# Issuing 64-row matmuls as two 64-column halves: a fused convolution and gated feed-forward kernel on one core

## The chip, the cores and the metric

The kernel runs on one core of a Trainium2 chip (trn2). The metric is the device time of one execution in microseconds. The kernel before takes 711.89 us, the median of two runs (711.63 and 712.15). One further execution was profiled. Engines are named as in the profile: PE is TensorE's matmuls, PEld its weight loads, DVE is VectorE, ACT is ScalarE, POOL is GpSimd, SP is SyncE, which here starts most transfers.

## What is computed

The input is x of 8 sequences by 4096 positions by 192 channels in fp32. First comes a causal convolution of 7 taps; the 192 channels fall into 8 heads of 24, and all channels of a head share 7 softmaxed taps. Its result, seen as 32768 tokens by 192, goes through a feed-forward layer with 2048 hidden units:

```
w   = softmax(weight, axis=-1)                        # 8 heads x 7 taps
a   = einsum('hk,bskhg->bshg', w, windows of 7 of x)  # causal, zero padded
h   = a.reshape(32768, 192) @ moe_w_in                # 192 x 2048
g   = h * cos(h)
out = g @ moe_w_out                                   # 2048 x 192, fp32
```

## The kernel before, in words

Everything is unrolled in Python, with the order of the instructions written out by hand (`manual_schedule`). Tokens are worked on in 64 tiles of T = 512 (index t); the convolution works in units of U = 1024 (index u), two tiles each. All matmul operands are bf16, and sums are fp32 in PSUM.

A matmul here has a stationary operand (`lhsT`, put into the array by a weight load, LDWEIGHTS) and a moving operand (`rhs`, streamed through). In almost all of the kernel a matmul uses only 64 of the array's 128 rows and all 128 columns. They come in pairs, one on rows 0 to 63 and one on rows 64 to 127, which write different PSUM banks. Such a pair is called a step below. There are three products made in this way:

- The convolution as a band matrix (`conv_mm`, L193, called by `conv_part`, L220). For units 3 and up each part is 8 matmuls of 64 rows, streaming 192 columns; units 1 and 2 use full 128-row matmuls through the same helper. Unit 0 has code of its own (`conv_first` L338, `conv_rest` L373), which the diff doesn't touch; it issues 128 by 128 matmuls that stream 48 columns (L347) or 96 (L379).
- The first layer (`mm1`, L402, matmul at L411). 192 channels are 3 blocks of 64. For each tile and each of 8 pairs j of hidden blocks there are 3 steps: k runs over the blocks, i over the two row halves, each half with its own hidden block and its own bank of the PSUM tile `h`. Each matmul streams 512 columns. ACT then takes the cosine (L419, by sine with a shift) and DVE multiplies (L423) into the SBUF tile `g`.
- The second layer (`mm2_step`, L430, matmul at L458). The stationary operand is a 64-row slice of `g` for 128 tokens, the moving one 64 rows of `wo` (192 columns). There are 64 steps per tile, and each step's two matmuls write the two banks of `o_ps`. After half of them the row halves change banks, with a `Turn` between (L163): `mark` puts a no-operation on SP's queue that depends on the last matmuls of the first half, and `wait` makes the first matmuls of the second half depend on it, so that two row halves never write one bank together. `conv_part` uses the same device.

The order on PE is a string for each tile, walked by the loop at the end. In the steady state it is

```
PE_ORDER = "m11 h0 m4 h1 m6 h2 m7 q Y K h3 m7 h4 m7 c1 m4 c2 X L m5 h5 m9 p h6 D O h7 m4"
```

where `h3` is the first-layer product j = 3, `m7` is seven steps of the second layer (of the tile before, mostly), and `c1`, `c2` are the two pieces of a convolution part. The other letters issue work on other queues: L loads x, K casts it, D doubles and X transposes by DMA, Y mends the edges of a unit, O stores. ACT and DVE follow in an order of their own (`ACT_ORDER`). PSUM's eight banks are all in use: three `h` tiles of two banks, and one bank each for `o_p` and `o_q`.

At the start PE is kept at work on a zero tile (`keep_warm`, L107) while the band matrix is built; after the first unit, PE runs the three products in turn until the end.

Of the kernel before, what the change touches and what calls it, by code (L numbers as in the profile page):

```python
# [16 lines left out]
def kernel(  # L17
# [8 lines left out]
    nc = tc.nc  # L26
# [3 lines left out]
    G = D // H  # L30
# [11 lines left out]
    NC = D // 64  # L42
# [37 lines left out]
    w = consts.tile([128, NC, NP, 128], BF16)  # L80
# [28 lines left out]
            nc.tensor.matmul(out=bank, lhsT=zero[:, 0:128], rhs=zero, start=True, stop=True)  # L109


    quarter = consts.tile([4, 128], FP32)
    nc.gpsimd.memset(quarter, 1.0)
    nc.gpsimd.affine_select(out=quarter, in_=quarter, compare_op=ALU.is_ge, fill=0.0, base=0, pattern=[[1, 128]],
# [19 lines left out]
    band = consts.tile([128, H, 256], BF16)  # L134
# [23 lines left out]
    wo = consts.tile([128, NP, 2, D], BF16)  # L158
# [18 lines left out]
    bf = {}  # L177
# [15 lines left out]
    def conv_mm(u, c, ps, i, rows, n0, n1, prev=0, **flags):  # L193

        h = 4 * c + i
        return nc.tensor.matmul(  # L196
            out=ps[i // 2][:, 0 : (n1 - n0) * 2 * G].rearrange("p (n k i r) -> p i n k r", n=n1 - n0, k=NC, i=2)[:, i % 2],
            lhsT=band[rows, h, 128 if prev else 0 : 256 if prev else 128],
            rhs=bf[u][rows, n0:n1, h * G : (h + 1) * G].rearrange("p n (k r) -> p n k r", k=NC),
            skip_group_check=True, **flags)  # L200

    def conv_out(u, c, ps, n0, m0, m1, copy, double=False, banks=(0, 1)):

        for b in banks:
            w0 = (2 * c + b) * 2 * R
            o = ct_tiles[u][:, m0:m1, :, :, w0 : w0 + 2 * R].rearrange("p n k t w -> p (n k) t w")
            i = ps[b][:, (m0 - n0) * 2 * G : (m1 - n0) * 2 * G].rearrange("p (m t w) -> p m t w", t=1, w=2 * R)
            if double:
                copy(o, i.to_broadcast([128, (m1 - m0) * NC, 2, 2 * R]))
            else:  # L210
                copy(o[:, :, 0, :], i[:, :, 0, :])  # L211

    def ring_banks():
        h = h_pool.tile([128, 2, T], FP32, name="h")
        return [h[:, 0, :], h[:, 1, :]]
# [4 lines left out]
    def conv_part(u, c, banks, whole=False):  # L220


        ps = banks()
        nb = UB + (u == 1)
        sides = [slice(0, 64), slice(64, 128)]

        def mm(i, rows, **flags):
            return conv_mm(u, c, ps, i, sides[rows], 0, nb, **{"start": False, "stop": False, **flags})

        if whole:  # L230
            for i in range(4):
                conv_mm(u, c, ps, i, slice(0, 128), 0, nb, start=i % 2 == 0, stop=i % 2 == 1)
            if u == 2 and c == 0:
                spread_taps(ps[1][:, UB * 2 * G : UB * 2 * G + K])
            yield
        else:
            mm(0, 0, start=True)
            mm(2, 1, start=True)
            turn = Turn()
            turn.mark(mm(1, 0), mm(3, 1))  # L240
            yield
            turn.wait(mm(2, 0), mm(0, 1))
            mm(3, 0, stop=True)
            mm(1, 1, stop=True)
        yield
        if u not in ct_tiles:
            ct_tiles[u] = ct_pool.tile([128, UB + 1, NC, 2, 64], BF16, name="ct")
        for b in range(2):
            conv_out(u, c, ps, 0, 0, nb, nc.scalar.copy, banks=(b,))
            if b and u == 2 and c == 0:  # L250
                nc.scalar.copy(tap, ps[1][:, UB * 2 * G : UB * 2 * G + K])
            if b:
                have.add(("conv", u, c))
            yield
# [28 lines left out]
    def spread_taps(ps):  # L283

        for i in range(2):
            nc.tensor.matmul(out=ps, lhsT=pick[:, i].rearrange("p t q i r -> p (t q i r)"), rhs=wn[:, i, :],
                             start=i == 0, stop=i == 1, skip_group_check=True)
# [40 lines left out]
    for i, k in enumerate("DPDPDPDPDPDPDPAA"):  # L328
        q, rows = divmod(i, 4)
# [69 lines left out]
    g_tiles = {}  # L399
    o_state = {}  # L400

    def mm1(t, j, n0=0, n1=NB):  # L402

        assert ("whole", t // TPU, t % TPU) in have
        c = cT[t // TPU]
        m0 = (t % TPU) * NB
        h = h_pool.tile([128, 2, T], FP32, name="h")
        for k in range(NC):
            for i in range(2):
                rows = slice(64 * i, 64 * i + 64)  # L410
                nc.tensor.matmul(out=h[:, i, n0 * 128 : n1 * 128], lhsT=w[rows, k, j, :], rhs=c[rows, m0 + n0 : m0 + n1, k, :],  # L411
                                 start=(k == 0), stop=(k == NC - 1))
        return h

    def gcu(t, j, h, n0=0, n1=NB):
# [14 lines left out]
    def mm2_step(q):  # L430
        tt, i = divmod(q, 2 * STEPS)
        half, k = divmod(i, STEPS)
        if tt >= NT:
            return
        if tt < NT - 1:
            f, si = divmod(k, 2)
            if i == 0:
                for b in range(2):
                    bank = o_pools[b].tile([128, T], FP32, name="o_ps%d" % b)
                    for j in range(2):  # L440
                        o_ps[tt, b, j] = bank[:, j * D : (j + 1) * D]
                    o_ps[tt, b] = bank[:, 0 : 2 * D]
            first, last = i == 0, i == 2 * STEPS - 1
        else:

            si, f = divmod(k, NF) if half else LAST_HALF[k]
            if half == 0 and f == 0:
                bank = [o_pools[b].tile([128, T], FP32, name="o_ps%d" % b) for b in range(2)] if si else ring_banks()
                for b in range(2):
                    o_ps[tt, b, si] = bank[b][:, 0:D]  # L450
            first, last = half == 0 and f == 0, half == 1 and f == NF - 1
        assert ("wo", f // 2 // HP) in have and {("g", tt, f // 2, s) for s in (2 * half + si, 2 * (1 - half) + si)} <= have
        ms = []
        for r in range(2):
            b = half ^ r
            rows = slice(64 * r, 64 * r + 64)
            s = 2 * b + si
            ms.append(nc.tensor.matmul(out=o_ps[tt, b, si], lhsT=g_tiles[tt][rows, f, s * 128 : (s + 1) * 128],  # L458
                                       rhs=wo[rows, f // 2, f % 2, :], start=first, stop=last, skip_group_check=True))
        if tt < NT - 1:  # L460
            if i == STEPS - 1:
                turns[tt] = Turn()
                turns[tt].mark(*ms)
            if i == STEPS:
                turns.pop(tt).wait(*ms)
        elif f == NF - 1 and half == 0:
            turns[tt, si] = Turn()
            turns[tt, si].mark(*ms)
        elif f == 0 and half == 1:
            turns.pop((tt, si)).wait(*ms)  # L470
# [18 lines left out]
    o_ps, o_sb, turns, evacs = {}, {}, {}, set()  # L489
# [21 lines left out]
    for v in (1, 2, 3):  # L511
        for i, part in enumerate("dc"):
            conv[part, v] = conv_part(v, i, ring_banks, v < 3)
    step, made, stored, done = 0, -1, 0, set()
    for t in range(NT + 1):
        u, second = divmod(t, TPU)
        cu = u + TPU
        if t >= 2 * TPU:
            conv["c"] = conv_part(cu, second, ring_banks) if cu < NU else iter(())
        pe = PE_LAST if t == NT - 1 else "m%d p" % (2 * STEPS * NT - step) if t == NT else PE_ORDER if t >= len(PE_FIRST) else PE_FIRST[t]  # L520
        act = ACT_LAST if t == NT - 1 else ACT_ORDER if t >= len(ACT_FIRST) else ACT_FIRST[t]
        act, h = act.split(), {}
# [35 lines left out]
        for k in pe.split():  # L558
            if k[0] == "h":
                if t < NT:  # L560
                    h[k[1:]] = mm1(t, int(k[1]), *HALVES[k[2:]])
            elif k[0] in "rdc":
                next(conv[part_of(k)], None)
            elif k[0] == "m":
                for q in range(step, step + int(k[1:])):
                    mm2_step(q)
                step += int(k[1:])
            elif k[0] == "w":
                keep_warm(int(k[1:]), o_pools[0].tile([128, T], FP32, name="o_ps0"))
            elif k == "p":  # L570
                assert step % (2 * STEPS) == 0
                made = step // (2 * STEPS) - 1
            elif k == "q":
                assert step % (2 * STEPS) == STEPS
            elif k[0] == "W":
                cast_wo(int(k[1]))
            elif k == "O":
                while stored <= made and (stored, 0) in evacs and (stored, 1) in evacs:
                    store(stored)
                    stored += 1  # L580
            elif k[1:]:
                of_unit(k[0], int(k[1]))
            else:
                v = {"D": cu, "X": u + 1, "Y": u + 1, "K": u + 3, "L": u + 4}[k]
                if t >= 2 * TPU and v < NU and (k in "DLY") == bool(second):
                    of_unit(k, v)
# [35 lines left out]
```

## Time and profile before

| what | value |
|---|---|
| median of the runs | 711.89 us |
| the profiled execution's own time | 711.61 us |
| its span in the profile | 709.9 us |
| mean granted TensorE clock | 0.999 |
| instructions in the span | 26545 |
| busy DVE, ACT, POOL | 637.5, 599.8, 304.2 us |

The span is the time from the program's first instruction to its last, and 1.7 us lie around it. PE's share of busy time is not a measure of how well it is used: a matmul's record is longer than the time after which the next can start, so records overlap and the row reads full even if they come less often. What counts is how far apart they start. The chain view gives that best: it lists runs of instructions of one kind with their number and the time until the next kind. In the lists of instructions the time given with several merged ones runs from the first start to the last end, so that the spacing is that time less one record, divided by one less than the number. "x14" is a count, and "64x192" the moving operand's rows by columns; "64*128" is rows by columns of the stationary operand.

### The profile page before, as it was taken

The numbers are of one execution on the slowest core, as the hardware profiler recorded it, in microseconds if no ns is written. First come the engines' busy times: TensorE is split into PE (matmuls) and PEld (weight loads), VectorE is DVE, ScalarE is ACT, GpSimd is POOL, SyncE is SP. The second block draws the span as 40 slices with busy tenths as digits, with TensorE's granted clock in tenths as the row PEclk, the third lists the DMA queues.
The fourth block names the chain that finished last, engine by engine and source line by source line (L and its number), as shares of the span: only waits on it lengthen the run. The fifth ranks groups of instructions, "written<-read, shape, count | busy, mean of one in ns | idle before, by whom it ended". The sixth has DMA issues, their size and how long they took to land.

```text
span 709.9 us, 26545 instructions
## 1 busy us (share of the span) xinstructions
PE 703.0 (99%) x11836; PEld 537.6 (76%) x11838; DVE 637.5 (90%) x598; ACT 599.8 (84%) x719; POOL 304.2 (43%) x308
## 2 busy tenths in 40 slices
PE   8999999999999999999999999999999999999997
PEld 4677777777777777777777777777777777777776
DVE  6889998998998999899999989989989999999996
ACT  7888888888888888888888888888888888888875
POOL 6653355333454433553434554335544335532400
PEclk9999999999999999999999999999999999999999
DMA  8954535535445455355354365553454554543411
GB/s 210 252 137 96 116 106 146 126 93 147 100 120 147 101 120 140 94 134 142 80 145 117 104 146 119 103 145 101 122 146 91 129 125 104 139 96 75 96 46 46
DMA packets 183713, 85.25 MB, mean 120 GB/s; under 512 B 111664, under 2 KB 183216, under 8 KB 183600
## 3 DMA queue, kind: packets, MB, share of 16 engines
q1 hardware_dynamic: 182888, 82.59, 47.9%
q8 instruction: 92, 1.51, 0.9%
q0 software_dynamic: 416, 0.79, 0.7%
q10 hardware_dynamic: 296, 0.20, 0.1%
q14 instruction: 21, 0.17, 0.1%
HBM read 31.36 MB, written 25.17 MB: 80 GB/s over the span
## 4 chain that ended last, share of the span: by engine, by line
PE 96%; DMA 1%; DVE 1%; POOL 0%; ACT 0%; SPq 0%; issue 0%; POOLq 0%
PE o_ps L458 47%; PE h L411 46%; PE h L196 3%; DMA x_f<-in_x_dram 1%; DVE g L423 0%; ACT cs L419 0%; PE h L458 0%; SPq L75 0%; POOL x_bf L184 0%; POOL mask L132 0%; PE o_ps L109 0%; ACT mask L137 0%; DVE diag L319 0%; DVE prod L316 0%; DVE o_sb L486 0%
## 5 line engine op out<-in xcount | busy, mean ns | idle before, releaser
L423 DVE TENSOR_TENSOR g<-h,cs 128x1024 bf16<-128x1024 f32 (+1 forms) x513 | 599.9, 1217 | 19.9 <-ACT cs L419 17.1
L419 ACT ACTIVATE cs<-h 128x1024 bf16<-128x1024 f32 (+1 forms) x513 | 514.4, 1022 | 85.1 <-PE h L411 64.9
L458 PEld LDWEIGHTS <-g 64*128 64x128 bf16 x8192 | 368.9, 94 | 91.6 <-DVE g L423 0.4
L458 PE MATMUL o_ps<-wo,g 64*128 64x192 bf16 x8128 | 434.8, 243 | 0.0
L411 PE MATMUL h<-cT,w 64*128 64x512 bf16 (+1 forms) x3078 | 412.2, 376 | 0.6 <-DVE g L423 0.3
L411 PEld LDWEIGHTS <-w 64*128 64x128 bf16 x3078 | 160.3, 94 | 67.4 <-issue 1.6
L302 POOL TENSOR_TENSOR edge_prod<-cT,tap 128x1008 f32<-128x1008 bf16 x30 | 67.2, 2241 | 281.7 <-DMA cT<-ct 281.7
L184 POOL CAST x_bf<-x_f 128x1728 bf16<-128x1728 f32 (+2 forms) x33 | 80.8, 2448 | 60.5 <-DMA x_f<-in_x_dram 42.3
L476 DVE COPY o_sb<-o_ps 128x384 f32<-128x384 f32 x62 | 34.6, 558 | 42.8 <-PE o_ps L458 42.6
L211 ACT CAST ct<-h 128x384 bf16<-128x384 f32 (+1 forms) x124 | 53.8, 484 | 14.0 <-PE h L196 13.4
L264 POOL COPY ct<-ct 128x1536 bf16<-128x1536 bf16 (+1 forms) x31 | 45.6, 1470 | 14.1 <-ACT ct L211 11.5
L196 PE MATMUL h<-x_bf,band 64*128 64x192 bf16 (+2 forms) x480 | 42.1, 243 | 0.1
L307 POOL TENSOR_TENSOR edge_prod<-edge_prod 128x144 f32<-128x144 f32 x60 | 33.3, 555 | 4.7
L305 POOL TENSOR_TENSOR edge_prod<-edge_prod 128x432 f32<-128x432 f32 x30 | 30.3, 1010 | 2.4
L476 ACT COPY o_sb<-o_ps 128x384 f32<-128x384 f32 x64 | 30.2, 474 | 0.1
L196 PEld LDWEIGHTS <-band 64*128 64x128 bf16 (+1 forms) x480 | 22.8, 94 | 1.5 <-issue 1.3
L308 POOL TENSOR_TENSOR cT<-edge_prod 128x144 bf16<-128x144 f32 x30 | 18.3, 610 | 2.4
L266 POOL COPY ct<-x_bf 128x192 bf16<-128x192 bf16 x60 | 19.2, 350 | 0.0
L109 PE MATMUL o_ps<-zero 128*128 128x512 bf16 x20 | 6.8, 476 | 1.4 <-DVE zero L104 1.3
L109 PEld LDWEIGHTS <-zero 128*128 128x128 bf16 x24 | 2.3, 110 | 4.2 <-issue 2.1
L93 POOL CAST wo<-wo_f 128x1536 bf16<-128x1536 f32 x2 | 2.9, 1469 | 2.4 <-DMA wo_f<-in_moe_w_out_dram 2.4
L458 PE MATMUL h<-wo,g 64*128 64x192 bf16 x64 | 3.2, 244 | 0.1
(61 smaller groups left out, 35.5 us busy)
## 6 DMA issues: line engine op xcount, KB each, us to landing
out_dram<-o_sb SPq DMA_DIRECT2D x63, 384.0 KB
x_f<-in_x_dram SPq DMA_DIRECT2D x30, 768.0 KB
x_f<-in_x_dram SPq DMA_DIRECT2D x31, 96.0 KB
x_f<-in_x_dram SPq DMA_DIRECT2D x4, 384.0 KB
wo_f<-in_moe_w_out_dram SPq DMA_DIRECT2D x4, 384.0 KB
w<-in_moe_w_in_dram POOLq DMA_DIRECT2D x2, 384.0 KB, 6.2
cT<-ct SPq DMA_TRANSPOSE x32
out_dram<-o_sb ACTq DMA_DIRECT2D x2, 96.0 KB
```

Of the source, the lines that this page charges most:

```text
L184: copy(out=bf[u][:, n0 + o : n1 + o, :].rearrange("p n (h k r) -> p (n h) k r", k=NC, r=R), in_=x_tiles[u][:, n0:n1, :].rearrange("p n (h ...
L196: return nc.tensor.matmul(out=ps[i // 2][:, 0 : (n1 - n0) * 2 * G].rearrange("p (n k i r) -> p i n k r", n=n1 - n0, k=NC, i=2)[:, i % 2], ...
L211: copy(o[:, :, 0, :], i[:, :, 0, :])
L264: nc.gpsimd.tensor_copy(out=ct[:, 0:nb, :, 1, :], in_=ct[:, 0:nb, :, 0, :])
L302: nc.gpsimd.tensor_tensor(out=edge_prod, in0=window, in1=tap.rearrange("p (a b k) -> p a b k", a=1, b=1).to_broadcast([128, NC * UB, K - 1 ...
L305: nc.gpsimd.tensor_tensor(out=edge_prod[:, :, :, 0:3], in0=edge_prod[:, :, :, 0:3], in1=edge_prod[:, :, :, 3:6], op=ALU.add)
L307: nc.gpsimd.tensor_tensor(out=edge_prod[:, :, :, 0], in0=edge_prod[:, :, :, 0], in1=edge_prod[:, :, :, j], op=ALU.add)
L411: nc.tensor.matmul(out=h[:, i, n0 * 128 : n1 * 128], lhsT=w[rows, k, j, :], rhs=c[rows, m0 + n0 : m0 + n1, k, :], start=(k == 0), stop=(k ...
L419: nc.scalar.activation(out=cs[:, :, part], in_=h[:, :, part], func=AF.Sin, bias=math.pi / 2.0, scale=1.0)
L423: nc.vector.tensor_tensor(out=g_tiles[t][:, 2 * j : 2 * j + 2, part], in0=h[:, :, part], in1=cs[:, :, part], op=ALU.mult)
L458: ms.append(nc.tensor.matmul(out=o_ps[tt, b, si], lhsT=g_tiles[tt][rows, f, s * 128 : (s + 1) * 128], rhs=wo[rows, f // 2, f % 2, :], star ...
L476: (copy or copies[b])(o_sb[t][:, 2 * b : 2 * b + 2, :].rearrange("p s d -> p (s d)"), o_ps.pop((t, b)))
```

## The change

A helper issues a matmul as two, on columns 0 to 63 and 64 to 127 of the stationary operand, writing partitions 0 to 63 and 64 to 127 of the same PSUM region; both stream the same moving operand. All three products call it. A step of two matmuls and two weight loads becomes four matmuls and four weight loads, each on a quarter of the array. The lists handed to `Turn` grow from two instructions to four. Nothing else changes: the order, the buffers, the transfers and the other engines' work stay.

```diff
+    COLS = [slice(0, 64), slice(64, 128)]
+
+    def halves_mm(out, lhsT, rhs, **flags):
+
+        return [nc.tensor.matmul(out=out[c], lhsT=lhsT[:, c], rhs=rhs, skip_group_check=True, **flags) for c in COLS]
...
     def conv_mm(u, c, ps, i, rows, n0, n1, prev=0, **flags):
 
         h = 4 * c + i
-        return nc.tensor.matmul(
-            out=ps[i // 2][:, 0 : (n1 - n0) * 2 * G].rearrange("p (n k i r) -> p i n k r", n=n1 - n0, k=NC, i=2)[:, i % 2],
-            lhsT=band[rows, h, 128 if prev else 0 : 256 if prev else 128],
-            rhs=bf[u][rows, n0:n1, h * G : (h + 1) * G].rearrange("p n (k r) -> p n k r", k=NC),
-            skip_group_check=True, **flags)
+        return halves_mm(
+            ps[i // 2][:, 0 : (n1 - n0) * 2 * G].rearrange("p (n k i r) -> p i n k r", n=n1 - n0, k=NC, i=2)[:, i % 2],
+            band[rows, h, 128 if prev else 0 : 256 if prev else 128],
+            bf[u][rows, n0:n1, h * G : (h + 1) * G].rearrange("p n (k r) -> p n k r", k=NC), **flags)
...
-            turn.mark(mm(1, 0), mm(3, 1))
+            turn.mark(*mm(1, 0), *mm(3, 1))
             yield
-            turn.wait(mm(2, 0), mm(0, 1))
+            turn.wait(*mm(2, 0), *mm(0, 1))
...
-                nc.tensor.matmul(out=h[:, i, n0 * 128 : n1 * 128], lhsT=w[rows, k, j, :], rhs=c[rows, m0 + n0 : m0 + n1, k, :],
-                                 start=(k == 0), stop=(k == NC - 1))
+                halves_mm(h[:, i, n0 * 128 : n1 * 128], w[rows, k, j, :], c[rows, m0 + n0 : m0 + n1, k, :],
+                          start=(k == 0), stop=(k == NC - 1))
...
-            ms.append(nc.tensor.matmul(out=o_ps[tt, b, si], lhsT=g_tiles[tt][rows, f, s * 128 : (s + 1) * 128],
-                                       rhs=wo[rows, f // 2, f % 2, :], start=first, stop=last, skip_group_check=True))
+            ms += halves_mm(o_ps[tt, b, si], g_tiles[tt][rows, f, s * 128 : (s + 1) * 128], wo[rows, f // 2, f % 2, :],
+                            start=first, stop=last)
```

## The prediction

> **What bounds the kernel now.** I read the page first (engines, clock, groups, instruction queue), then the chain of waits in a steady stretch, then the list of instructions where PE issues most densely.
>
> ```profile
> PE 703.0 (99%) x11836; PEld 537.6 (76%) x11838; DVE 637.5 (90%) x598; ACT 599.8 (84%) x719; POOL 304.2 (43%) x308
> ...
> PEclk9999999999999999999999999999999999999999
> ...
> q8 instruction: 92, 1.51, 0.9%
> ...
> L458 PEld LDWEIGHTS <-g 64*128 64x128 bf16 x8192 | 368.9, 94 | 91.6 <-DVE g L423 0.4
> L458 PE MATMUL o_ps<-wo,g 64*128 64x192 bf16 x8128 | 434.8, 243 | 0.0
> L411 PE MATMUL h<-cT,w 64*128 64x512 bf16 (+1 forms) x3078 | 412.2, 376 | 0.6 <-DVE g L423 0.3
> ```
>
> PE stands idle before its two big groups for 0.0 and 0.6 us in 709.9, at full clock throughout. Busy alone proves little, since a record (243 or 376 ns) is longer than the spacing. The chain gives the spacing, first as a whole, then in a window:
>
> ```profile
> 128.82 1.29 PE h L411 x12
> 139.61 1.29 PE h L411 x12
> ...
> 665.28 1.32 PE o_ps L458 x32
> ```
>
> ```profile
> 130.12 1.24 PE o_ps L458 x30
> 131.36 0.65 PE h L411 x6
> ```
>
> 32 matmuls of L458 are 16 steps in 1.32 us, 82.5 ns for a step that streams 192 columns (15 steps in 1.24 agree). 6 of L411 are 3 steps in 0.65 us, about 216 ns for 512 columns. The same place of the order comes round after 139.61 - 128.82 = 10.79 us, one tile: 24 steps of L411, 64 of L458 and 4 of L196. 68 x 82.5 = 5.61 us leave 5.18 for the 24, 215.8 ns each. The difference is 133.3 ns for 320 columns, 0.4166 ns each; so 512 columns are 213.3 ns, 192 are 80.0, and each step has 2.5 ns on top. The two row halves stream side by side, at one column per 0.4166 ns each, and all 128 columns of the array are in use. The period holds nothing but steps: PE's streaming is the bound, and the weight loads (94 ns each as recorded) are fully under it.
>
> Over the whole kernel there are 3072 / 2 = 1536 steps of L411 and 8192 / 2 + 464 / 2 = 4328 steps of 192 columns (L458 and L196). 1536 x 215.8 + 4328 x 82.5 = 331.5 + 357.1 = 688.6 us; the other 21.3 us of the span are start and end. The profiled execution took 711.6 us, 0.3 below the median of the runs, so sums against it hold for the median too.
>
> **The change, part by part.**
>
> *Streaming.* Removed: 11728 matmuls in 5864 steps. Added: 23456, four to a step, each on a quarter of the array, each streaming as many columns as before. If the four stream side by side as the two do now, a step costs what it did, 215.8 or 82.5 ns: nothing won, nothing lost. No row shows two column halves at work, so the ends are: below nothing, the fixed 2.5 ns of a step gone (-14.7 us); above, the column halves of a row half one after the other (+688.6). I take 0: two row halves overlap fully now, and quarters are nearest to that.
>
> *Issue.* A step's 2 loads and 2 matmuls become 4 and 4; at 192 columns that is a load and a matmul each 82.5 / 4 = 20.6 ns, against 41.2 now. The densest place is in the prologue:
>
> ```profile
> 8.30 0.56 PE L347 MATMUL o_ps<-x_bf,band 128*128 128x48 bf16 x16
> ```
>
> Here each matmul has a load of its own and streams 48 columns, 48 x 0.4166 + 2.5 = 22.5 ns; 0.56 us less one record of 0.183, over 15, is 25.1 ns. So one pair of load and matmul after the other on the same part of the array takes no less than about 25.1. On different parts the starts are closer:
>
> ```profile
> 12.54 0.39 PE L411 MATMUL h<-cT,w 64*128 64x512 bf16 x2 [0.30 <-DVE g L423]
> 12.54 0.11 PEld L411 LDWEIGHTS <-w 64*128 64x128 bf16 x3 [0.58 <-issue]
> ```
>
> Two matmuls of the two row halves lie within 0.39 us, one record being 0.376: at most 14 ns apart; three loads start within 0.11 - 0.094, about 16 ns. The 25.1 ns is therefore no spacing that the whole array keeps, and counted for a row half alone it is 2 x 25.1 = 50.2 ns, under 82.5. In front of PE, where instructions are fetched and decoded, the mean counts: 23456 x 25.1 = 588.7 us, still under 688.6. I take 0; the upper end is the rival below (+77.5 us). The steps of 512 columns have 215.8 / 4 = 54 ns a pair and bear either reading.
>
> The Trainium skill, "TensorE: Matmul & The Clock Gate", Part 1, says that the spacing of matmul starts never falls below about 25 ns. For one part of the array the 25.1 ns agrees; for two row halves the 14 ns does not.
>
> *Instruction fetch.* PE's 1.51 MB in 92 packets doubles to about 3 MB, 1.8% of the DMA engines: hidden, as they are fetched ahead (a packet each 7.7 us now, 3.9 then); not hidden, each wait would show as PE idle ended by "issue".
>
> *Weight loads.* Each covers 64 columns instead of 128, with twice as many. Now they hide: one per row half in 82.5 ns, while a pair in the L347 row shows that a load of 128 columns can pass in 25.1. Two half-width loads per row half are at most 2 x 25.1 = 50.2 ns, under 82.5, so 0. If they are not hidden, each step pays one load in front of its matmul: 12.5 ns (half of 25.1) to 94 ns (a whole record), x 5864 = 73 to 551 us.
>
> *Turns and waits.* The SP no-operation now depends on four matmuls instead of two, and the first four of the other half on it. In PE's order the last comes at most one quarter later, some 20 ns; behind the no-operation on SP's queue stand loads of x, stores and transposes, which have microseconds to spare, and each `Turn` has another block of matmuls between mark and wait. 0; without that cover some 120 turns x 20 ns, 2.4 us. ACT and DVE wait for the last quarter of `h`, which ends when the pair did. The 16 full-row matmuls of units 1 and 2 become 32, at most 16 x 25.1 = 0.4 us.
>
> Sum: 711.6 + 0.4 = 712 us, the same within what can be measured.
>
> **The rivals.**
>
> *A floor under issue over the whole array.* If the 25.1 ns of the L347 row hold for any pair once the quarters share rows, a 192-column step is 4 x 25.1 = 100.4 ns, +17.9 x 4328 = +77.5: 789 us. It speaks for this that no row shows pairs denser than 41.2 ns sustained; against it, the 14 ns above. It decides (over 2%) from 21.5 ns a pair, 85.8 a step.
>
> *Weight loads show.* Loads of half the columns that are slower, or that pass one at a time for the four quarters. At 25.1 unhidden in each step: +147, 859 us; at the ends above, 785 to 1263. For it: four loads instead of two must pass in 82.5 ns, and nothing in the trace is a 64-column load. Against it: row-half loads start within 16 ns of each other and PE never waits for one.
>
> The Trainium skill, "TensorEngine Tiling (Array Packing)", Restrictions, says that column tiling turns Fast Weight Load off, which speaks against this change. With the load time of its page "TensorE: Matmul & The Clock Gate", section LDWEIGHTS (columns / 1.2 ns, so 53 ns for 64), four in a row would be 213 ns a step, and the time, an estimate from that page, about 1277 us; side by side they would hide and the time stays 712. No row here shows which.
>
> *Column halves take turns.* If two matmuls on the same rows cannot stream together, every step doubles: 711.6 + 688.6 = 1400 us. Only the lack of any row speaks for it.
>
> *Faster.* If the fixed 2.5 ns of a step are hidden by the other column half, 5864 x 2.5 = 14.7 us go: 697 us, 2.1% less. It needs nearly all of it. The next engine, DVE with 637.5, leaves room; but the 2.5 ns are there today with two row halves at work, so overlap has not removed them so far.
>
> **How the numbers follow.** Forecast 0.42: 712, own range 708 to 726. Floor under issue 0.25: 726 to 789. Weight loads 0.24: 785 to 1263, a little over half of it below 870. Column halves in turn 0.06: about 1400. Faster 0.03: 697. The forecast is the likeliest single case, but the slower cases together hold 0.55, because three things that no row shows must all go well. 2% (14 us) is about what a measurement of this kernel can tell from no change: faster 0.03, same 0.42, slower 0.55. The range that leaves out 2 in 10 runs from 706 to 870: it loses the faster case, the upper part of the loads (0.11) and the turns (0.06).
>
> **What would show it.** Right: about 23,600 matmuls and as many loads; the chain's runs keep their times at double counts (L411 x24 in 1.29 us, L458 x60 in 1.24), and the period stays 10.79 us. Issue floor: L411's spacing unchanged, L458's step near 100 ns, period about 12.0 us, no load late. Loads: L411's steps lengthen too, or PE starts stand right behind loads. Turns: L411's step near 430 ns. Wrong altogether if DVE or ACT become slower per instruction, or the granted clock falls below 1.

## The result, and the profile after

The changed kernel takes 784.05 us, median of two runs (783.44 to 784.66), against 711.89 before: a ratio of 1.1014, 95% interval 1.0966 to 1.1061. It is 10% slower. The profiled execution took 784.66 us, with a span of 783.0 and a mean granted clock of 0.995; the span grew by 73.1 us. Of all executions of the experiments below one was slow as a whole (749.40 us, without the transposes), and its median leaves it out.

From the page of the profile after (the helper's line is now L116):

```profile
PE 724.0 (92%) x23586; PEld 611.7 (78%) x23588; DVE 645.4 (82%) x598; ACT 600.4 (77%) x719; POOL 304.6 (39%) x308
...
q8 instruction: 184, 3.01, 1.6%
...
PE 91%; issue 7%; DVE 1%; ACT 1%; POOL 0%; POOLq 0%
...
L116 PE MATMUL o_ps<-wo,g 64*64 64x192 bf16 x16256 | 469.5, 244 | 33.8 <-issue 33.3
L116 PEld LDWEIGHTS <-g 64*64 64x64 bf16 x16384 | 423.6, 107 | 93.0 <-issue 44.4
L116 PE MATMUL h<-cT,w 64*64 64x512 bf16 (+1 forms) x6156 | 438.5, 377 | 18.7 <-issue 16.6
```

The counts have doubled, as they should. New is the idle time of PE, 33.8 and 18.7 us before groups that had 0.0 and 0.6, nearly all ended by "issue": PE waited for no semaphore that the profile shows. The chain has 7% of it where it had 0%. Its window over a bad stretch, in start, time and count:

```profile
479.39 1.29 PE h L116 x24
480.68 1.24 PE o_ps L116 x60
481.92 0.65 PE h L116 x12
482.57 0.33 PE o_ps L116 x16
482.89 0.38 PE h L116 x6
483.28 1.82 issue
485.10 0.49 PE h L116 x5
```

Until 482.89 every run takes exactly what it took before with half the count: 24 matmuls in 1.29 us, 60 in 1.24. The quarters stream side by side at full rate, and the doubled loads are hidden. Then, in the middle of a first-layer product (it breaks off after 6 matmuls of 12), PE has nothing for 1.82 us.

Where do these breaks lie? Over the whole trace, from the starts of single instructions: 70 stretches over 0.25 us without a new load or matmul after the first 25 us, together 71.5 us, nearly all of the 73.1. Of these, 62 with 68.9 us lie whole multiples of 256 of PE's instructions apart, its semaphore instructions counted. PE's instruction queue (q8) moved 3.01 MB in 184 packets of 16 KB for 47,174 loads and matmuls: 64 bytes an instruction, 256 instructions a packet. Such a packet's instructions are called a page here, so PE runs out at the border of a page. One packet is seen for each page; its timing, from the starts of packets and instructions:

| from | to | us, median |
|---|---|---|
| PE's first instruction of a page | start of the next page's packet, nothing else moving (105 of 181 pages) | 1.06 |
| the same, right behind DMA transposes | | 2.06, at most 3.97 |
| the same, among loads and stores | | 2.0, at most 3.61 (in the start-up once 4.47) |
| start of the packet | its end | 1.07 |
| end of the packet, where PE stands | PE's first instruction of that page | 1.38 |

Undisturbed that is 1.06 + 1.07 + 1.38 = 3.5 us from one page to the next. A page now lasts 256 / 736 x 10.79 = 3.75 us on average (736 loads and matmuls a tile), against 7.5 before. What disturbs it shows in windows of the changed kernel, one with a transpose and a quiet one (the last column but one is the share of the DMA engines' time, the last GB/s):

```profile
478.40:482.60 4.20, 4.20 (x149) 3.67 (x144) 3.43 (x5) 3.45 (x5) 0.00 (x0) 1.00 1.10 209
...
470.00:478.00 8.00, 6.98 (x241) 6.30 (x235) 6.86 (x7) 5.45 (x7) 2.56 (x1) 1.00 0.08 24
```

For 4.2 us the DMA engines are full with one transpose of `cT` in 256-byte packets; the page packet that PE needs starts at 482.85, when the last of these are through, ends at 483.78, and PE goes on at 485.10.

### The profile page after: what moved, and what is told of

Same layout as the page of the kernel before. It is cut to its first block, busy times and chain, and to the rows that moved or that the text cites. A ratio compares the mean times of both kernels' runs of the same rounds, so it can differ in the third digit from the quotient of the medians.

```text
span 783.0 us, 50045 instructions
## 1 busy us (share of the span) xinstructions
PE 724.0 (92%) x23586; PEld 611.7 (78%) x23588; DVE 645.4 (82%) x598; ACT 600.4 (77%) x719; POOL 304.6 (39%) x308
## 3 DMA queue, kind: packets, MB, share of 16 engines
q8 instruction: 184, 3.01, 1.6%
## 4 chain that ended last, share of the span: by engine, by line
PE 91%; issue 7%; DVE 1%; ACT 1%; POOL 0%; POOLq 0%
PE h L116 46%; PE o_ps L116 44%; DVE g L428 1%; ACT cs L424 0%; PE o_ps L109 0%; DVE band L335 0%; POOL mask L138 0%; ACT mask L143 0%; ACT ct L358 0%; PE o_ps L384 0%; DVE diag L324 0%; DVE cT L376 0%; PE o_ps L352 0%; PE h L373 0%; DVE prod L321 0%
## 5 line engine op out<-in xcount | busy, mean ns | idle before, releaser
L428 DVE TENSOR_TENSOR g<-h,cs 128x1024 bf16<-128x1024 f32 (+1 forms) x513 | 607.9, 1218 | 80.8 <-ACT cs L424 76.7
L424 ACT ACTIVATE cs<-h 128x1024 bf16<-128x1024 f32 (+1 forms) x513 | 514.5, 1021 | 154.3 <-PE h L116 142.5
L116 PE MATMUL o_ps<-wo,g 64*64 64x192 bf16 x16256 | 469.5, 244 | 33.8 <-issue 33.3
L116 PEld LDWEIGHTS <-g 64*64 64x64 bf16 x16384 | 423.6, 107 | 93.0 <-issue 44.4
L116 PE MATMUL h<-cT,w 64*64 64x512 bf16 (+1 forms) x6156 | 438.5, 377 | 18.7 <-issue 16.6
L116 PEld LDWEIGHTS <-w 64*64 64x64 bf16 x6156 | 214.9, 107 | 63.2 <-issue 26.6
L116 PE MATMUL h<-x_bf,band 64*64 64x192 bf16 (+2 forms) x960 | 48.5, 245 | 0.4
L116 PEld LDWEIGHTS <-band 64*64 64x64 bf16 (+1 forms) x960 | 27.6, 106 | 2.8 <-issue 2.6
L116 PE MATMUL h<-wo,g 64*64 64x192 bf16 x128 | 3.5, 245 | 0.3 <-issue 0.2
```

The costliest lines, as they stand in the source:

```text
L116: return [nc.tensor.matmul(out=out[c], lhsT=lhsT[:, c], rhs=rhs, skip_group_check=True, **flags) for c in COLS]
L424: nc.scalar.activation(out=cs[:, :, part], in_=h[:, :, part], func=AF.Sin, bias=math.pi / 2.0, scale=1.0)
L428: nc.vector.tensor_tensor(out=g_tiles[t][:, 2 * j : 2 * j + 2, part], in0=h[:, :, part], in1=cs[:, :, part], op=ALU.mult)
```

## The experiments

The theory after this reading: PE runs out of instructions, since a page's packet waits behind bursts of data and a page now lasts hardly longer than its fetch. Rivals: column halves cost something of their own; a page is simply too slow, whatever else moves; the price belongs to doubling as such. Times are medians; ratios are of means, against the kernel before on the same chip. In the lists of waits a break can stand twice, once for the loads (PEld) and once for the matmuls (PE).

**Twice the matmuls without column halves.** In all three products, here the second layer:

```diff
+        for d0 in (0, D // 2):
-                ms.append(nc.tensor.matmul(out=o_ps[tt, b, si], ... rhs=wo[rows, f // 2, f % 2, :], start=first, ...
+                ms.append(nc.tensor.matmul(out=o_ps[tt, b, si][:, d0 : d0 + D // 2], ...
+                                           rhs=wo[rows, f // 2, f % 2, d0 : d0 + D // 2], start=first and d0 == 0, ...
```

> Row halves as before, no column halves; each matmul of all three products is issued twice, for half of its streamed columns each (256 and 256, 96 and 96), so that PE gets as many instructions as the changed kernel. Theory (PE runs out of instructions, whose 16 KB pages come late): PE's streaming is 688.6 us plus one more 2.5 ns per step, 14.7, so 726 without stalls; with page waits of 45 to 75 us on top, 770 to 800 us, idle PE ended by 'issue' every 256 instructions. Rival (column halves cost something of their own): 726 us and no such idle time.

Measured: 786.48 us, ratio 1.1039 (1.1003 to 1.1075). Its list of waits, in us, times and longest:

```profile
PEld L463 <- issue: 33.5, 32, 2.5
PE o_ps L463 <- issue: 29.0, 27, 2.3
PEld L415 <- issue: 18.6, 16, 2.3
PE h L415 <- issue: 12.7, 11, 2.0
```

With no 64 by 64 matmul in it, this kernel has waits of the same kind, all but one of its breaks at the border of a page, and about the same time. So column halves are not needed for the waits; the number of instructions is part of the cause. The sums differ: here the breaks come to 52.2 us, against 71.5 in the changed kernel, and the added steps have a price of their own, which a later run shows.

**The transposes replaced by a plain copy on POOL.** In the changed kernel, from unit 2 on, so that the values behind it are others:

```diff
-        nc.sync.dma_start_transpose(out=cT[u][:, n0:n1].rearrange("p n c k -> p (n c) k"), ...
+        nc.gpsimd.tensor_copy(out=cT[u][:, n0:n1].rearrange("p n c k -> p (n c k)"), ...
```

> The changed kernel, with the DMA transposes from unit 2 on replaced by a plain copy on POOL, so that no transfer is made there (left out: the transposition, so the values that follow are others). Theory (a page waits behind the transposes): the 28 waits that follow a transpose, 34.9 us in all, go, those after loads and stores (24.7 us) stay: about 749 us, between 735 and 760. Rival (a page takes about 3.3 us to come whatever else moves): 780 to 785 us.

Measured: 739.28 us, ratio 1.0378 (1.0339 to 1.0416), with single runs from 735.2 to 741.2. Some 45 us go with the transposes, 10 more than the 34.9 us of waits that directly follow one. The rival of the slow page (780 to 785) falls.

**The same bytes in large packets.**

```diff
-        nc.sync.dma_start_transpose(...
+        nc.sync.dma_start(out=cT[u][:, n0:n1].rearrange("p n c k -> p (n c k)"), ...
```

> The changed kernel, with the DMA transposes from unit 2 on replaced by a plain DMA copy of the same bytes in large packets (left out: the transposition). If a page waits for all that is queued ahead of it, a copy that takes as long as the transpose costs the same, 775 to 785 us; if it waits only for the packets or the time of the burst, less: 740 to 765 us.

Measured: 760.77 us, ratio 1.0700 (1.0670 to 1.0729). The transposes' bytes alone account for about half of their price; their many small packets, or the longer burst, for the rest. This run can't separate these two.

**The control.** The same copy on POOL in the kernel before.

> Control: the kernel before with the same copy on POOL in place of the DMA transposes (left out: the transposition). PE's streaming is the bound and pages come every 7.6 us, so every theory here says 712 us, within 2.

Measured: 712.04 us, ratio 1.0005 (0.9995 to 1.0015). Without doubled instructions the transposes cost nothing.

**No transfers at all.** The changed kernel with the copy on POOL, and:

```diff
-                load_unit(v)
-                load_edges(v)
+                if v < 6:
+                    load_unit(v)
+                    load_edges(v)
+                else:
+                    x_tiles[v] = x_tiles[v - 2]
...
-                    store(stored)
+                    if stored < 4:
+                        store(stored)
```

> The changed kernel with hardly any data moved in the steady state: no DMA transposes from unit 2 on (a copy on POOL instead), no loads of x from unit 6 on (older tiles are used again), no stores between tile 3 and the last (left out: all that, so most of the output is not written). Theory (a page waits behind data transfers; alone it comes within 3.4 us, and the mean page lasts 3.75): 712 to 722 us with the same 23,600 matmuls. Rival (pages are simply too slow for 736 instructions per 10.79 us): still 735 to 745 as with the loads and stores.

Measured: 716.39 us, ratio 1.0066 (1.0051 to 1.0081). Page and chain of this run:

```profile
PE 704.9 (99%) x23588; PEld 599.4 (84%) x23588; DVE 637.6 (89%) x598; ACT 599.6 (84%) x719; POOL 396.3 (55%) x338
```

```profile
306.03 1.29 PE h L116 x24
307.32 1.24 PE o_ps L116 x60
308.56 0.65 PE h L116 x12
```

All quarter matmuls are there, the runs follow each other without a break, and 67.7 of the 72.2 us are gone. Most of what is left is one wait of 2.6 us at 38.4 us, while the start-up transfers still run. Pages that come undisturbed are fast enough.

**Loads and stores away, transposes kept.**

> The changed kernel with its DMA transposes kept, but no loads of x from unit 6 on (older tiles are used again) and no stores between tile 3 and the last (left out: those, so most of the output is not written). Taking the transposes away saved 44 us, all transfers together 68. If the two kinds of burst hold up different pages, loads and stores are worth the rest, some 24 us: 755 to 765 us. If they hold up the same pages, less is saved: 770 to 784.

Measured: 751.53 us, ratio 1.0549 (1.0506 to 1.0593). Loads and stores are worth 32.5 us, transposes 45, both together 67.7: they hold up mostly different pages, with some 10 us in common. Single runs of this kernel differ by 6 us, so the part in common is rough.

**The other doubling without transfers.**

> Row halves with the streamed columns split in two (as in the first experiment), with hardly any data moved in the steady state: no DMA transposes from unit 2 on, no loads from unit 6 on, no stores between tile 3 and the last (left out: all that). Theory: the 2.5 ns of each added step remain, 14.7 us, and the page waits go: 724 to 732 us. Rival (row halves in smaller pieces lose by other means): 750 or more.

Measured: 731.38 us, ratio 1.0276 (1.0260 to 1.0291). That is 15.0 us above the column halves without transfers: the split of the streamed columns has a price of its own, near the 14.7 us of the added 2.5 ns. The other 55 us of the first experiment go with the transfers, as the waits of the column halves did.

**A longer page.** The streamed columns are split in the second layer and the convolution only.

> No column halves; the streamed columns split in two in the second layer and the convolution only, the first layer as before. 640 matmuls and loads per tile: 256 last 4.4 us. PE's streaming grows by 4328 x 2.5 ns = 10.8 us to 722 without stalls. Theory: page waits between those of the changed kernel (page 3.75 us, some 70 us) and of the kernel before (7.6 us, none): 20 to 45 us, so 740 to 768. Rival (a fixed price of doubling): 722.

Measured: 729.11 us, ratio 1.0245 (1.0228 to 1.0262). 7 us over the 722 without waits, less than I expected: ten breaks, 6.8 us together. In the first experiment, with the same kind of split in all products, a page lasts 3.8 us, and the breaks counted in the same way are 45 with 52.2 us. A page of 4.4 us has 0.9 of margin over the 3.5 of an undisturbed fetch, one of 3.8 has 0.3.

**The same bytes, spread.** The transposes of the changed kernel, in three pieces:

```diff
-    PE_ORDER = "... c1 m4 c2 X L m5 h5 m9 p h6 D O h7 m4"
+    PE_ORDER = "... c1 m4 c2 U L m5 h5 m4 V m5 p h6 D O h7 Z m4"
+            elif k in "UVZ":
+                turn_unit(v, 3 * "UVZ".index(k), 3 * "UVZ".index(k) + 3)
```

> The changed kernel, with each DMA transpose from unit 3 on issued in three pieces of three blocks, at three places of the tile some 2.5 us apart, so that no burst of them lasts much over 1.4 us. Same bytes, same matmuls. Theory: a page behind a piece starts at most 1.4 us late and PE waits at most about 1 us for it; the waits after transposes fall from 34.9 us to 5 to 15, those after loads and stores stay: 755 to 768 us. Rival (what counts is how much is moved, not how long a burst holds a page up): 780 to 785.

Measured: 768.85 us, ratio 1.0803 (1.0787 to 1.0819), 15 us better and just above the forecast. Waits behind transposes fell from 34.9 to 20.1 us, not to 15: there are now more of them (30 for 28), each shorter. The length of a burst counts, but not alone.

**Column halves in the first layer only.**

> Column halves in the first layer only, the other two products as before. 464 matmuls and loads per tile, so 256 of them last 5.95 us on average. Theory: a page behind a burst of 4.2 us is late by at most 3.4 + 4.2 - 5.95 = 1.7 us, and mostly not: 712 to 725 us. Rival, for this run alone: going to and fro between 64 by 128 and 64 by 64 some 14 times a tile empties the array each time; at 0.1 us each that is 90 us more, 800 us, with steps lengthened at the borders and no page waits.

Measured: 813.74 us, ratio 1.1431 (1.1414 to 1.1448): worse than all three products. This is its own rival, not pages. Waits and chain:

```profile
PEld L464 <- issue: 183.4, 447, 0.4
PEld L116 <- issue: 71.2, 446, 0.6
```

```profile
305.63 0.85 PE o_ps L464 x18
306.48 1.42 PE h L116 x24
307.90 1.34 PE o_ps L464 x30
```

Each run is about 0.1 us longer than before (1.42 for 1.29, 1.34 for 1.24), and 893 waits, none over 0.6 us, stand at the changes from one product to another: 102.2 us of added span over 893 is 0.114 us for going from 128 columns to 64 or back. The Trainium skill, "TensorEngine Tiling (Array Packing)", Key Properties, says that a change of tiling mode drains the array; the time lost at each change in this run agrees, though the trace does not show the drain itself.

**Two attempts on the kernel before**, to make page waits appear with the old number of instructions. A second transpose right behind each:

> The kernel before, with each DMA transpose from unit 2 on made a second time into a spare tile right behind the first, so that the burst lasts some 8.4 us instead of 4.2. Nothing waits for the second. Theory: a page that is asked for early in the burst is now late by up to 3.4 + 8.4 - 7.6 = 4.2 us, about one in two bursts: page waits appear in the kernel before, 10 to 40 us, so 722 to 752. Rival (pages are late only because PE has twice as many instructions): 712.

Measured: 748.18 us, ratio 1.0511 (1.0488 to 1.0533). Inside the forecast, and for another reason:

```profile
PEld L462 <- SPq L168: 45.6, 29, 2.5
PE o_ps L462 <- SPq L168: 31.7, 28, 2.0
```

PE waits for SP's no-operation of the `Turn` (L168), which stands on SP's queue behind the second transpose; that one keeps SP for 4.36 us (median). Of the 43.6 us of breaks in this trace 42.1 end with that no-operation, and they do not lie multiples of 256 instructions apart, so the number says nothing for the theory. Then loads from POOL's queue instead:

```diff
+            for spare in spares:
+                nc.gpsimd.dma_start(out=spare, in_=xf[0:U, :].rearrange("(n p) d -> p n d", p=128))
```

> The kernel before, with two more loads of 768 KB into spare tiles started from POOL's queue right behind each DMA transpose from unit 2 on, so that the burst of transfers is longer while SP's queue isn't held up. Nothing waits for them. Theory: only a page that starts more than 7.6 - 2.5 = 5.1 us after it is asked for makes PE wait, and the latest start seen behind loads in the changed kernel is 4.7; so few waits, 712 to 728 us, and those that come end by 'issue' at a page border. Rival (row-half kernels have no page waits at all, whatever the burst): 712, with no idle PE ended by 'issue'.

Measured: 746.12 us, ratio 1.0472 (1.0455 to 1.0490), above both forecasts. The waits are again those of the `Turn`, among others:

```profile
PEld L462 <- SPq L168: 27.6, 25, 1.9
PEld L415 <- issue: 16.5, 19, 1.5
PE o_ps L462 <- SPq L168: 15.5, 19, 1.5
PE h L415 <- POOL cT L312: 12.5, 15, 1.3
```

Again the breaks do not lie multiples of 256 instructions apart. Those of L415 stand, but for a few, where a matmul waits for POOL to mend the edges of `cT`; the loads beside it are put down to "issue". Both kinds point at the transposes on SP's queue, L276 in this run and L275 in the kernel before (ns, shortest, median and longest):

```profile
L276 SPq DMA_TRANSPOSE cT<-ct x32: 3838/8309/9372, 16.0 to 698.8; - x32
...
L275 SPq DMA_TRANSPOSE cT<-ct x32: 3102/4210/5741, 16.0 to 663.6; - x32
```

Beside the spare loads a transpose keeps SP for twice as long, although these are on another queue; the no-operation behind it comes late, and so does `cT`. One such case: a transpose keeps SP from 312.33 us for 8.94, a store follows until 321.90, and PE's wait for the no-operation ends at 322.01. Whether a burst that is long enough would starve the kernel before of instructions stays open: neither run shows it.

## Why the prediction was right or wrong

The range (706 to 870) holds 784, and "slower" had the largest chance. The forecast itself, 712 and no change, was wrong. That the range reached so far is luck: it did so for a floor under issue and for weight loads, and neither came.

- *Streaming, 0:* right. 24 matmuls in 1.29 us and 60 in 1.24 are the old steps of 215.8 and 82.5 ns.
- *Issue, 0:* right. Loads and matmuls come every 10.3 ns on average in a 192-column step with no floor in sight.
- *Weight loads, 0:* right. Their record is 107 ns instead of 94, and it is hidden. They cost nothing measurable. The Trainium skill, "TensorEngine Tiling (Array Packing)", Restrictions, has Fast Weight Load off in this form; no run here shows whether it is, only that nothing waits for it.
- *Turns and waits, 0:* right; the waits of the changed kernel for the no-operation of a `Turn` (now L174) are one of 0.2 us.
- *Instruction fetch, 0:* this step failed. I wrote that it is "hidden, as they are fetched ahead (a packet each 7.7 us now, 3.9 then)", and weighed the bytes, 1.8% of the DMA engines. What counts is time: 3.5 us from page to page undisturbed, against 3.75 that a page lasts, and up to 2.9 us more behind transposes and 2.6 among loads and stores (once, in the start-up, 3.4). It cost 67.7 us. The signature was named rightly (PE idle, ended by "issue"), but it had no price and no chance.
- *The rival nearest in time*, a floor under issue at 789 us, was wrong in its mechanism: it asked for 100.4 ns a step and a period near 12.0 us everywhere, and the chain has 82.5 with breaks between. A time that fits a rival does not prove it; its signature must be there too.
- *The sign of being wrong altogether*, a granted clock below 1, did come, but for a short time (last section): worth at most 3.3 us (0.11 of 30). DVE and ACT kept their times (1218 ns for 1217, 1021 for 1022).

Enough was in the profile before to price it. 0.9% of 16 engines' 709.9 us over 92 packets is 1.1 us a packet; 92 packets give a page's length, and half of it is 3.8 us; the window of a transpose, here in the kernel before, shows some 4 us with the DMA engines full:

```profile
300.50:304.70 4.20, 4.20 (x75) 3.24 (x72) 3.43 (x5) 3.45 (x6) 0.00 (x0) 1.00 1.10 212
```

If a packet is asked for only when the page before it begins, one that waits 4 us and takes 1.1 does not come within 3.8.

The Trainium skill, "Runtime: NRT & Kernel Launch", Instruction fetch mechanics, has the fetch in 16 KB blocks of 256 instructions, which the trace shows. It also calls the crossing of a block mostly hidden, since instructions are issued more slowly than blocks arrive. At 14.7 ns an instruction (10.79 us / 736) and with other transfers this is not so: 716 us without them, 784 with them.

## What to carry to other kernels

Doubling the instructions of a busy engine can cost without any of them being slow: compare the time in which the engine uses up 256 instructions with the time in which the next page comes, and add the longest burst of other transfers. Where PE is idle with "issue", look for the number of instructions between the breaks before blaming matmuls. And if array tiles are split, split all of a stretch or nothing, as each change of shape cost 0.114 us here.

## What the runs showed of the hardware

Splitting both rows and columns into four 64 by 64 quarters streams neither faster nor slower than two halves (24 matmuls take the 1.29 us that 12 took, 60 the 1.24 that 30 took). A packet of instructions has no right of way: it started up to 2.9 us late behind transposes and 2.6 among loads and stores. A DMA transpose keeps SP's queue for 4.2 us (median) in the kernel before, and for 8.3 beside the spare loads. And in the windows of the changed kernel the granted clock (the third number from the end) is 0.89 between 30 and 60 us, where PE has its longest break (3.7 us, at 37.9), and 1.00 there in the kernel before. That the break is the cause is likely, and was not tried; its length alone does not decide, since a break of 2.6 us at this place left the clock at 1.00 without transfers, and one of 2.2 went with 0.94 in the other doubling without transfers:

```profile
30.00:60.00 30.00, 26.52 (x792) 21.91 (x786) 20.43 (x20) 19.82 (x27) 10.78 (x12) 0.89 0.55 133
60.00:100.00 40.00, 38.23 (x1263) 32.30 (x1252) 35.59 (x33) 33.30 (x41) 14.18 (x13) 1.00 0.48 109
```
